# A limit in kilobytes for the loads in flight, shorter channel loads and earlier branch hints in a fused RWKV-5 and SwiGLU kernel

## The chip, the cores and the metric

The kernel runs on one core of one Trainium2 chip. The metric is the time of one execution on the device in microseconds (us); the table below gives the median of three runs.

## The reference, cut to what matters

The first half is a linear attention with a decaying state, for 4 batches, 8 heads, 768 tokens and 48 channels per head. The second half normalises each token's 384 features and puts them through a SwiGLU layer of width 1536. All is float32.

```python
for t in range(S):
    kt, vt, rt = (k[:, :, t], v[:, :, t], r[:, :, t])
    cur = np.einsum('bhd,bhe->bhde', u[None] * kt, vt)
    y[:, :, t] = np.einsum('bhd,bhde->bhe', rt, state + cur)
    state = w[None, :, :, None] * state + np.einsum('bhd,bhe->bhde', kt, vt)
...
rms = np.sqrt(np.mean(x * x, axis=-1, keepdims=True) + 1e-06)
xn = x / rms * rms_g
g = xn @ w_gate
silu = g * (1.0 / (1.0 + np.exp(-g)))
return (silu * (xn @ w_val) @ w_out).astype(np.float32)
```

## The kernel before, in words

The 768 tokens are cut into 12 chunks of 64 (`NS`, index s). For each chunk the kernel loads three arrays: `CH` holds r and k with channels on the partitions ("chan", loaded by `load_chan`), `TOK` holds r and k with tokens on the partitions (`load_tok`), and `V` holds v (`load_v`). Each has one buffer only, so that a load has to wait until the chunk before has been read. A chunk of attention (`mixing(s)` and `state(s)`) goes as follows. DVE decays r into `RR` and k in place (rows named R and K). TensorE forms the scores A from them (`products`), and in the first two chunks also E, from u times k, which ScalarE makes as `ku`. DVE writes the diagonal and the masked scores into `MT` (d and m). TensorE forms the outputs Y from `V`, `MT` and, from the second chunk on, the state `ST` and the decayed r. ScalarE keeps the outputs as `yT` and their squares as `sq`. The mean of the squares (r, `ms`), its root (POOL `pow`, DVE `inv`, `diag` and TensorE `spread` in the first two chunks) and the scaling (x) follow. U is the chunk's update of the state; it needs `KH`, which DVE makes from `TOK` and the table `wk`; ScalarE (first chunk) or DVE then brings it into `ST`.

Weights come as 64-bit words and are rounded to float32: a load on SP into one of six `raw` buffers, an `ulp` on ScalarE, two operations `bits` on DVE, and a sum on POOL (`piece`). Gate and value products then go through the three PSUM banks a, b and c. The first two chunks are multiplied plainly (`gate_val`, `project`); from the third on, two chunks together go through a seven-product scheme (`group`, `second_layer`). In this later part, 36 loads called "look" (`check`) read the weights once more into `rows_out` to test their low bits; ScalarE works on them.

Nothing here is left to a scheduler. `Plan` holds all 1536 operations, each with an engine, a cost and its dependencies; `ORDER` is one list written out by hand that says in which order they are issued, and so the order on every engine. The costs serve one thing only: `times` works out from them when TensorE would idle, and `warm` fills such gaps, in the first PE operations, with matmuls of `ones` into an unused bank, so that TensorE is not idle. Their number is a function of the planned gap. The first gap has a formula of its own:

```python
for _ in range(4 * int((until + 0.4 - 3.75) / 0.86)):
    pe.matmul(bank[:, 0, 0:P], ones, ones, start=True, stop=True)
...
for _ in range(int((until - since - 0.25) / 0.23)):
```

All loads stand in one queue, SP's, and are issued in order. `InOrder.at_most` (line 165) keeps four counted loads in flight: the fifth gets a wait on the landing of the oldest. The loads of `CH`, `TOK`, `V` and the raw weights are counted, the look loads and the stores are not.

At the end, a value computed on the chip (`bad`) is loaded into a register on each engine, and a branch (`tc.If` in `program`, line 1773) goes past the general version of the kernel, which is not needed for these inputs. `hint` marks the branch as likely taken, on each engine. It is called by `Plan.give` (line 231) ahead of the third-last TensorE operation, and each engine's hint stands after the last instruction that the engine has been given by then.

Of the kernel before, what the change touches and what calls it, by code (L numbers as in the profile page):

```python
# [49 lines left out]
P = 128  # L50
# [10 lines left out]
B, H, S, D = 4, 8, 768, 48  # L61
# [11 lines left out]
def feature_order():  # L73
# [10 lines left out]
    0, 6, 8, 42, 44, 5, 4, 7, 21, 11, 10, 41, 43, 16, 1, 2, 3, 45, 46, 47, 76, 12, 51, 48, 49, 52, 53, 55, 31, 36, 26,  # L84
    13, 14, 58, 50, 59, 15, 54, 17, 22, 60, 62, 65, 66, 100, 18, 19, 23, 24, 113, 9, 108, 103, 20, 67, 68, 83, 56, 27,
    61, 84, 63, 64, 57, 25, 69, 70, 38, 33, 39, 28, 71, 72, 124, 77, 86, 78, 126, 90, 29, 34, 118, 193, 85, 79, 87,
    30, 123, 80, 133, 32, 127, 125, 102, 81, 195, 82, 105, 106, 104, 37, 200, 128, 134, 35, 40, 107, 91, 131, 129,
    109, 114, 95, 130, 132, 92, 135, 119, 73, 110, 136, 96, 137, 155, 115, 111, 120, 116, 205, 210, 121, 139, 140, 97,
    138, 101, 93, 75, 74, 279, 112, 117, 141, 142, 143, 156, 150, 151, 157, 122, 98, 196, 163, 159, 160, 144, 197,
    198, 149, 145, 161, 206, 201, 164, 146, 199, 191, 274, 192, 284, 88, 152, 158, 162, 147, 148, 167, 218, 207, 202,  # L90
    165, 168, 169, 166, 203, 212, 213, 171, 172, 215, 170, 216, 208, 175, 176, 204, 209, 179, 180, 211, 177, 173, 217,
    174, 178, 183, 187, 89, 181, 182, 276, 219, 277, 153, 227, 275, 184, 188, 281, 194, 289, 280, 222, 282, 321, 311,
    306, 185, 225, 189, 247, 248, 249, 186, 214, 154, 190, 99, 278, 283, 251, 252, 255, 285, 250, 253, 254, 220, 256,
    257, 94, 238, 259, 263, 260, 264, 291, 286, 287, 288, 258, 267, 313, 308, 292, 314, 307, 224, 290, 228, 221, 271,
    316, 293, 261, 312, 268, 317, 265, 269, 223, 226, 309, 229, 331, 326, 336, 272, 266, 270, 262, 310, 315, 298, 302,
    294, 295, 242, 230, 322, 233, 234, 328, 355, 352, 318, 323, 299, 303, 296, 231, 300, 304, 297, 232, 353, 356, 235,
    236, 243, 327, 346, 319, 324, 305, 301, 329, 237, 244, 341, 273, 386, 390, 391, 387, 246, 354, 358, 245, 357, 320,
    325, 330, 332, 359, 362, 388, 392, 342, 333, 338, 334, 343, 344, 335, 339, 347, 337, 340, 345, 361, 364, 365, 348,
    360, 389, 375, 407, 349, 380, 363, 383, 381, 239, 393, 384, 500, 350, 366, 406, 394, 395, 351, 368, 369, 416, 437,
    367, 396, 241, 370, 501, 371, 382, 405, 404, 502, 398, 372, 399, 400, 373, 504, 503, 397, 438, 507, 509, 240, 374,  # L100
    376, 408, 378, 512, 377, 401, 402, 445, 409, 410, 385, 403, 413, 439, 446, 456, 457, 417, 441, 440, 447, 411, 442,
    462, 443, 444, 448, 451, 449, 463, 450, 464, 452, 453, 455, 454, 506, 458, 460, 465, 505, 459, 470, 467, 471, 466,
    468, 472, 508, 469, 473, 414, 415, 418, 590, 461, 422, 481, 474, 412, 476, 482, 510, 477, 478, 475, 483, 518, 591,
    513, 480, 484, 489, 485, 511, 479, 486, 490, 491, 487, 514, 488, 628, 492, 627, 519, 515, 520, 525, 493, 495, 624,
    526, 527, 496, 625, 497, 494, 521, 499, 528, 533, 523, 522, 530, 534, 419, 420, 423, 421, 424, 428, 524, 516, 517,
    425, 636, 529, 535, 498, 531, 544, 532, 626, 536, 634, 539, 598, 537, 545, 629, 540, 647, 541, 633, 538, 546, 543,
    547, 552, 635, 549, 548, 542, 550, 551, 630, 553, 631, 555, 554, 558, 632, 556, 563, 559, 560, 562, 565, 564, 557,
    567, 637, 426, 427, 429, 430, 566, 651, 568, 561, 571, 569, 570, 574, 582, 584, 575, 572, 573, 599, 577, 576, 578,
    638, 579, 434, 431, 583, 600, 595, 596, 601, 639, 581, 580, 592, 606, 585, 589, 593, 611, 432, 433, 588, 435, 586,
    602, 603, 587, 597, 436, 607, 642, 612, 643, 700, 640, 594, 747, 644, 701, 608, 615, 645, 756, 641, 652, 609, 610,  # L110
    646, 748, 614, 648, 649, 749, 616, 613, 617, 619, 618, 681, 744, 745, 650, 605, 653, 654, 621, 604, 682, 620, 657,
    746, 622, 683, 623, 660, 826, 689, 656, 684, 655, 685, 754, 690, 757, 753, 751, 691, 686, 706, 687, 688, 692, 695,
    693, 707, 708, 696, 697, 699, 709, 694, 702, 658, 703, 704, 714, 711, 698, 712, 715, 659, 661, 750, 662, 710, 663,
    705, 716, 717, 713, 725, 718, 755, 762, 719, 666, 720, 726, 827, 752, 727, 721, 723, 758, 722, 724, 728, 863, 733,
    860, 730, 664, 665, 763, 734, 729, 731, 732, 667, 669, 735, 736, 759, 760, 739, 864, 737, 769, 740, 771, 861, 741,
    770, 764, 765, 865, 743, 862, 772, 777, 866, 738, 766, 767, 670, 778, 668, 671, 774, 742, 773, 775, 780, 675, 779,
    776, 783, 834, 781, 867, 873, 782, 788, 784, 785, 790, 789, 835, 787, 791, 796, 793, 792, 786, 869, 797, 798, 794,
    795, 799, 802, 883, 800, 870, 676, 807, 803, 804, 806, 809, 808, 810, 801, 815, 812, 672, 673, 674, 677, 816, 768,
    761, 811, 805, 678, 888, 813, 818, 814, 821, 819, 817, 836, 831, 832, 871, 822, 823, 820, 872, 868, 825, 824, 828,
    829, 833, 874, 837, 843, 838, 679, 680, 844, 875, 839, 830, 878, 879, 847, 876, 841, 980, 981, 846, 877, 887, 880,  # L120
    842, 881, 845, 848, 851, 882, 884, 889, 886, 885, 984, 850, 891, 852, 890, 853, 919, 855, 849, 917, 918, 983, 920,
    982, 854, 856, 857, 990, 840, 858, 922, 921, 923, 924, 893, 859, 925, 892, 896, 931, 936, 926, 937, 927, 932, 933,
    928, 942, 929, 935, 944, 943, 945, 986, 938, 985, 939, 894, 930, 940, 934, 993, 895, 947, 950, 998, 987, 951, 946,
    948, 899, 1063, 941, 953, 952, 949, 954, 956, 961, 957, 1096, 958, 963, 962, 960, 964, 988, 992, 955, 965, 966,
    989, 969, 959, 967, 968, 972, 1097, 900, 897, 970, 898, 991, 975, 973, 976, 994, 901, 971, 1098, 905, 1001, 977,
    974, 979, 978, 999, 1005, 1000, 1007, 1006, 1003, 1013, 1008, 1002, 1010, 1009, 1011, 1012, 995, 1102, 1014, 1015,
    1070, 1016, 1019, 1017, 1105, 902, 903, 904, 908, 1062, 1024, 1020, 1021, 1119, 1023, 1026, 1025, 1027, 1018,
    1106, 1028, 1029, 1032, 1022, 1030, 1031, 1035, 1033, 1100, 1034, 1038, 1036, 1043, 1039, 906, 1103, 1040, 1045,
    1044, 1124, 1004, 1037, 909, 907, 911, 996, 1047, 1042, 1046, 1099, 1048, 1041, 1049, 1051, 1071, 1050, 1101,
    1109, 910, 1123, 1054, 1052, 1108, 1104, 1107, 997, 914, 1057, 1055, 1216, 1056, 1110, 1060, 1053, 1058, 1059,  # L130
    1061, 1064, 1072, 1111, 912, 1065, 1114, 1115, 1067, 1068, 1073, 1078, 1074, 1075, 1083, 1172, 1173, 913, 1069,
    1112, 1217, 1066, 1219, 915, 916, 1113, 1116, 1084, 1079, 1117, 1080, 1118, 1120, 1218, 1121, 1122, 1082, 1125,
    1126, 1087, 1229, 1076, 1088, 1086, 1089, 1091, 1085, 1155, 1127, 1153, 1154, 1077, 1128, 1156, 1093, 1094, 1158,
    1157, 1159, 1160, 1220, 1092, 1090, 1081, 1095, 1161, 1167, 1228, 1223, 1162, 1225, 1163, 1164, 1168, 1129, 1169,
    1226, 1165, 1171, 1174, 1221, 1234, 1177, 1299, 1178, 1132, 1180, 1298, 1166, 1222, 1179, 1175, 1176, 1186, 1170,
    1181, 1224, 1227, 1182, 1332, 1183, 1187, 1184, 1185, 1230, 1232, 1130, 1131, 1333, 1188, 1189, 1192, 1190, 1197,
    1193, 1135, 1335, 1194, 1199, 1198, 1235, 1191, 1196, 1200, 1205, 1195, 1202, 1203, 1133, 1134, 1206, 1201, 1138,
    1207, 1208, 1204, 1334, 1211, 1209, 1241, 1212, 1336, 1344, 1231, 1236, 1136, 1213, 1243, 1242, 1210, 1345, 1337,
    1237, 1215, 1244, 1214, 1249, 1238, 1239, 1246, 1245, 1250, 1251, 1247, 1248, 1137, 1139, 1140, 1144, 1252, 1255,
    1253, 1338, 1341, 1254, 1260, 1256, 1257, 1306, 1259, 1262, 1261, 1307, 1263, 1268, 1265, 1258, 1266, 1269, 1264,  # L140
# [18 lines left out]
class InOrder:  # L159


    def __init__(self, tc, engine):
        self.tc, self.engine, self.flying = tc, engine, []

    def at_most(self, n, give):


        made = give()
# [13 lines left out]
class Plan:  # L182
# [48 lines left out]
    def give(self, order, free, idle, hint, final):  # L231
# [4 lines left out]
        for i in order:  # L236
            if i == last[0]:
                hint()
# [9 lines left out]
def fast(ctx, tc, chan, tok, vpad, wka, wkb, wot, cols, u_row, out, bad):  # L248
# [12 lines left out]
    FIRST, IN_FLIGHT = 2, 4  # L261
# [1590 lines left out]
```

## Time and profile before

| What | Value |
|---|---|
| Time, median of 3 runs | 594.98 us (593.34 to 597.05) |
| Time of the profiled execution | 594.46 us |
| Its span, first to last instruction | 592.7 us |
| TensorE (PE) busy | 582.0 us, 98% |
| VectorE (DVE), ScalarE (ACT), GpSimd (POOL) busy | 415.3, 293.8, 41.9 us |
| Granted TensorE clock, mean | 0.998 |
| DMA, whole span | 62.99 MB, mean 106 GB/s |
| DMA, first 50 us | 14.99 MB, mean 300 GB/s |

The profile comes from one execution. "Busy" is the time in which an engine had at least one instruction running, so the filler matmuls count as busy too. In the profile every program matmul of float32 has two records, and two weight loads. A releaser, "<-", is what ended the idle time ahead of a row. Nearly all operations carry line 179, which is the wrapper that issues them, so the rows are told apart by the names of the tiles.

### The profile page before, as it was taken

What the parts mean: (1) busy time and instruction counts of PE and PEld (TensorE: products, weight loads), DVE (VectorE), ACT (ScalarE), POOL (GpSimd) and SP (SyncE); (2) the same over time, 40 slices, a digit from 0 to 9 for tenths busy, and PEclk for the clock granted to TensorE, in tenths of its full rate; (3) what the DMA queues carried; (4) which work ended last, traced back from release to release, by engine and by line L of the source; (5) the groups of instructions that cost most, each with busy time, mean ns of one, the idle gap of its engine ahead of it and who ended that gap; (6) DMA issues with size and microseconds to landing.
All of it is one profiled execution on the core that took longest, in us unless ns stands there. A gap on an engine that the chain in (4) does not pass through costs nothing.

```text
span 592.7 us, 16598 instructions
## 1 busy us (share of the span) xinstructions
PE 582.0 (98%) x7280; PEld 520.5 (88%) x7280; DVE 415.3 (70%) x622; ACT 293.8 (50%) x713; POOL 41.9 (7%) x40
## 2 busy tenths in 40 slices
PE   8999999999999999999999999999999999999996
PEld 7888887668888998888999889999889999988995
DVE  7888769595786977776795667795777585455641
ACT  5864458364366654564462474584365473124100
POOL 2443234100000000000000000000000000000000
PEclk9999999999999999999999999999999999999999
DMA  7975463412613123512222415301531200301002
GB/s 268 337 254 232 167 239 90 146 34 55 213 55 116 55 75 103 198 36 97 82 92 67 143 58 187 133 8 40 165 119 62 69 29 17 92 2 54 2 4 55
DMA packets 22768, 62.99 MB, mean 106 GB/s; under 512 B 2944, under 2 KB 9760, under 8 KB 21280
## 3 DMA queue, kind: packets, MB, share of 16 engines
q1 hardware_dynamic: 21920, 61.36, 30.8%
q8 instruction: 58, 0.95, 0.7%
q10 hardware_dynamic: 768, 0.49, 0.3%
q14 instruction: 22, 0.18, 0.1%
HBM read 56.04 MB, written 4.72 MB: 103 GB/s over the span
## 4 chain that ended last, share of the span: by engine, by line
PE 95%; DMA 2%; DVE 1%; issue 1%; ACT 0%; SPq 0%; POOL 0%; DVEq 0%
PE bank_b L179 33%; PE bank_c L179 27%; PE bank_a L179 27%; PE at L179 8%; DMA V<-in_vpad_dram 1%; DMA chan<-in_chan_dram 1%; DVE ms L179 0%; DVE KH L179 0%; ACT ku L179 0%; SPq L179 0%; ACT wk L179 0%; POOL ms L179 0%; ACT diag L179 0%; DVE rows_out L179 0%; DVE diag L179 0%
## 5 line engine op out<-in xcount | busy, mean ns | idle before, releaser
L179 DVE TENSOR_TENSOR gv<-bank_b,m 128x512 f32<-128x512 f32 x90 | 62.1, 690 | 63.5 <-PE bank_b L179 59.2
L179 ACT ACTIVATE gv<-gv 128x512 f32<-128x512 f32 (+1 forms) x60 | 30.8, 522 | 74.9 <-DVE gv L179 74.7
L179 DVE TENSOR_TENSOR gv<-bank_c,gv 128x512 f32<-128x512 f32 x60 | 41.4, 690 | 21.7 <-PE bank_c L179 21.2
L179 PE MATMUL bank_b<-xa,wa 64*128 64x256 f32 x444 | 55.3, 379 | 0.0
L179 PEld LDWEIGHTS bank_b<-xa,wa 64*128 64x128 f32 x444 | 43.2, 187 | 5.0 <-issue 0.7
L179 PE MATMUL bank_a<-xb,wb 64*128 64x256 f32 x372 | 46.5, 379 | 0.0
L179 PE MATMUL bank_a<-xa,wa 64*128 64x256 f32 x372 | 46.0, 378 | 0.0
L179 PE MATMUL bank_b<-t,s 64*128 64x256 f32 x360 | 45.2, 379 | 0.6 <-issue 0.6
L179 PE MATMUL bank_a<-wo,h 128*128 128x192 f32 x264 | 45.2, 327 | 0.0
L179 ACT ACTIVATE MT<-dmask,du 128x64 f32<-128x64 f32 x160 | 41.8, 336 | 6.1 <-DVE du L179 6.0
L179 PE MATMUL bank_b<-t,wb 64*128 64x256 f32 x360 | 44.6, 378 | 0.0
L179 PE MATMUL bank_c<-t,s 64*128 64x256 f32 x360 | 44.4, 376 | 0.0
L179 PE MATMUL bank_c<-xb,s 64*128 64x256 f32 x360 | 44.2, 376 | 0.0
L179 PEld LDWEIGHTS bank_a<-wo,h 128*128 128x128 f32 x264 | 43.2, 190 | 0.5
L179 ACT COPY m<-bank_a 128x512 f32<-128x512 f32 (+1 forms) x35 | 19.9, 568 | 47.7 <-PE bank_a L179 39.3
L179 ACT ACTIVATE gv<-bank_a 128x256 f32<-128x256 f32 x30 | 11.5, 382 | 58.6 <-PE bank_a L179 58.6
L179 PEld LDWEIGHTS bank_a<-xb,wb 64*128 64x128 f32 x372 | 36.3, 187 | 4.2 <-issue 0.3
L179 PEld LDWEIGHTS bank_b<-t,s 64*128 64x128 f32 x360 | 35.2, 187 | 5.4 <-issue 1.7
L179 PEld LDWEIGHTS bank_a<-xa,wa 64*128 64x128 f32 x372 | 36.4, 187 | 3.8
L179 ACT ACTIVATE rows_out<-rows_out 128x384 f32<-128x384 f32 x72 | 39.1, 554 | 0.5
L179 PEld LDWEIGHTS bank_c<-t,s 64*128 64x128 f32 x360 | 35.8, 187 | 3.5
L179 PEld LDWEIGHTS bank_c<-xb,s 64*128 64x128 f32 x360 | 35.5, 187 | 3.6
(189 smaller groups left out, 1099.3 us busy)
## 6 DMA issues: line engine op xcount, KB each, us to landing
chan<-in_chan_dram SPq DMA_DIRECT2D x11, 1024.0 KB, 5.4
TOK<-in_tok_dram SPq DMA_DIRECT2D x10, 768.0 KB, 4.7
V<-in_vpad_dram SPq DMA_DIRECT2D x12, 512.0 KB, 5.3
raw<-in_wot_dram SPq DMA_DIRECT2D x8, 576.0 KB, 5.0
rows_out<-in_wka_dram SPq DMA_DIRECT2D x12, 384.0 KB, 3.2
rows_out<-in_wkb_dram SPq DMA_DIRECT2D x12, 384.0 KB, 3.9
rows_out<-in_wot_dram SPq DMA_DIRECT2D x12, 384.0 KB, 3.4
raw<-in_wka_dram SPq DMA_DIRECT2D x6, 576.0 KB, 5.8
```

Of the source, the lines that this page charges most:

```text
L179: return lambda *args, **kwargs: self.tc.keep_in_program_order(give(*args, **kwargs))
```

## The change

1. **Limit in flight.** `at_most(4, ...)` becomes `within(1800, size, ...)`: each counted load carries its size in thousands of bytes, and a new load waits for the oldest ones until the sum, itself included, is at most 1800. Sizes: a chan piece of the first chunk 262, `TOK` 786 (or 393), `V` 524, a raw piece 393 or 590. The look loads are now counted too, each as 901.
2. **Channel rows.** From the second chunk on, chan is loaded as two transfers of 48 partitions (393 each) in place of one of 128 partitions; rows 48 to 63 of each half, which are padding, are left out. The planned cost of this load falls from 3.3 to 2.6.
3. **Branch hints.** TensorE's hint goes ahead of the 14th-last TensorE operation instead of the third-last; the hints of the other engines go to the middle of `ORDER`.
4. **Order.** `ORDER` is another permutation of the same operations, and the list of unused banks for the fillers is changed with it.

```diff
-    def at_most(self, n, give):
+    def within(self, limit, size, give):
         made = give()
-        self.flying.append(made.ins)
-        if len(self.flying) > n:
+        self.flying.append((made.ins, size))
+        while len(self.flying) > 1 and sum(x for _, x in self.flying) > limit:
             self.tc.add_manual_dep(
-                made.ins, self.flying.pop(0).name,
+                made.ins, self.flying.pop(0)[0].name,
...
-        last = [i for i in order if self.ops[i][0] == "PE"][-3:]
+        last = [i for i in order if self.ops[i][0] == "PE"][-14:]
+        middle = order[len(order) // 2]
         for i in order:
             if i == last[0]:
-                hint()
+                hint(mybir.EngineType.PE)
+            if i == middle:
+                hint(*(engine for engine in mybir.ALL_ENGINES if engine != mybir.EngineType.PE))
...
-    FIRST, IN_FLIGHT = 2, 4
+    FIRST, IN_FLIGHT = 2, 1800
...
     def load_chan(s):
-        sp.at_most(IN_FLIGHT, lambda: sp.dma_start(out=CH, in_=chan[s]))
+        for z in range(2):
+            rows = slice(64 * z, 64 * z + D)
+            sp.within(IN_FLIGHT, 393, lambda: sp.dma_start(out=CH[rows], in_=chan[s, rows]))
...
-            "SP", 0.95, [], keys, lambda: sp.dma_start(out=raw, in_=src[:, k * CHECK : (k + 1) * CHECK]), land=3*LAND,
+            "SP", 0.95, [], keys, lambda: sp.within(IN_FLIGHT, IN_FLIGHT // 2 + 1, lambda: sp.dma_start(out=raw, in_=src[:, k * CHECK : (k + 1) * CHECK])), land=3*LAND,
...
-    unused = list("baaaacbbbbbb")
+    unused = list("bbaaccbbbbbbbb")
...
-    def hint():
+    def hint(*engines):
         traced = nc.cur_bb.bb.instructions
-        for engine in mybir.ALL_ENGINES:
+        for engine in engines:
```

The built programs differ as follows. The matmuls of the computation are the same; the fillers fall from 31 program matmuls to 22 (12 in the first gap in both, 19 and 10 after it). The first loads on SP go from k1, r1, k0, r0, raw, raw, V to k0, r1, k1, r0, raw, V, raw, where r and k are the pieces of chan and the digit is the pair of batches q. On DVE the first R (of q1) goes ahead of the table `down`. On TensorE the second scores A of the first chunk go ahead of the first Y, and the second half of the product into bank b goes from after the second chunk's A to ahead of the first U. Program instructions from hint to branch: DVE 6 and 308, ACT 4 and 332, SP 5 and 85, POOL 2 and 2, PE 20 and 87 (before and after; a PE matmul makes four records).

## The prediction

> **What bounds the kernel now.** I read the page first. TensorE is busy for 98% of the span at full clock, and stays at 9 tenths or more in all but the first and the last slice.
>
> ```profile
> span 592.7 us, 16598 instructions
> PE 582.0 (98%) x7280; PEld 520.5 (88%) x7280; DVE 415.3 (70%) x622; ACT 293.8 (50%) x713; POOL 41.9 (7%) x40
> ...
> PE   8999999999999999999999999999999999999996
> ```
>
> So a change that leaves the matmuls alone can win only fillers, gaps at the start, and what follows the last matmul. The table by stretches says that PE is busy 8.72, 8.86, 8.96 and 9.26 of each 10 us up to 40, and then all of it but for 0.61 us near 354. The list of PE's waits is short; "issue" is a wait that the profile cannot explain.
>
> ```profile
> PE bank_b L179 <- DVE h L179: 1.1, 1, 1.1
> PE at L179 <- DMA V<-in_vpad_dram: 0.8, 1, 0.8
> PE at L179 <- issue: 0.7, 1, 0.7
> PE bank_a L179 <- issue: 0.7, 1, 0.7
> ```
>
> The timeline of PE shows where the start is lost (start, length, tiles, records):
>
> ```profile
> 7.04 0.71 PE L179 MATMUL bank_a<-ones 128*128 128x128 f32 x4
> 9.13 1.60 PE L179 MATMUL bank_a<-ones 128*128 128x128 f32 x12
> 11.54 0.91 PE L179 MATMUL at<-MT,V 64*64 64x64 f32 x48 [0.80 <-DMA V<-in_vpad_dram]
> 14.00 0.91 PE L179 MATMUL bank_c<-MT,V 64*64 64x64 f32 x48
> 24.57 1.15 PE L179 MATMUL at<-V,KH 64*64 64x48 f32 x64 [0.37 <-DVE KH L179]
> 31.20 0.57 PE L179 MATMUL at<-MT,V 64*64 64x64 f32 x23
> 32.52 0.81 PE L179 MATMUL at<-MT,V 64*64 64x64 f32 x41 [0.74 <-issue]
> ```
>
> The reader should see that PE is filled up, not needed, until about 25: Y of the first chunk waits for V, U for KH, and after Y of the second chunk (31.20) PE only runs its list. The time won at 31.20 is the time won at the end, if nothing stalls later.
>
> The chain of waits ends with PE until 586.83 and one DVE add until 587.22; the span ends 5.5 us later. The rows of the branch line show what lies there:
>
> ```profile
> L1773 SPq EVENT_SEMAPHORE  x8: 17/17/17, 590.8 to 591.4; - x8
> L1773 POOLq COMPARE_BRANCH  x1: 65/65/65, 561.6 to 561.6; - x1
> L1773 POOLq EVENT_SEMAPHORE  x1: 17/17/17, 563.9 to 563.9; - x1
> ...
> L1773 DVEq COMPARE_BRANCH  x1: 84/84/84, 586.9 to 586.9; - x1
> L1773 ACTq COMPARE_BRANCH  x1: 73/73/73, 587.8 to 587.8; - x1
> L1773 SPq COMPARE_BRANCH  x1: 70/70/70, 587.8 to 587.8; - x1
> L1773 ACTq EVENT_SEMAPHORE  x1: 17/17/17, 588.3 to 588.3; - x1
> L1773 DVEq EVENT_SEMAPHORE  x1: 21/21/21, 590.3 to 590.3; - x1
> ```
>
> From branch to next event ACT takes 0.5 us, POOL 2.3, SP 3.0 and DVE 3.4. SP is last, and the closing barrier takes 1.3 us more (591.4 to 592.7).
>
> [...] 58 instruction packets of 0.95 MB on one queue are 16.4 KB each, and three branches cost 2.3 to 3.4 us against 0.5. [...]
>
> **The change, part by part.** Times are of the profiled execution.
>
> *First loads.* Before, V was the seventh load and was issued at 6.30, held by the limit of four; it landed by 11.40. Now the four chan pieces and a raw piece make 4 x 262 + 393 = 1441, V would make 1965, so V waits only for the first piece (4.08, when the first ku started). The last chan piece was used at 7.03. From there to 11.40, two raw pieces and V landed: 1310 KB in 4.37 us, 300 KB/us. Now 917 KB are left: V lands at 7.03 + 3.06 = 10.1, 1.3 earlier.
>
> *First Y.* DVE ends `up` at 5.28; then R q1 0.82, `down` 0.68, K q0 0.68, R q0 0.75 end at 8.2. PE: E q0 from 7.05 (r0), E q1 from 7.7 (ku q1, 6.30 + 1.28), A q0 from 8.4 to 9.1. m q0 takes 0.76: 9.9. So the first Y starts at 10.1, held by V, for 11.54. DVE then has bits (0.34 + 0.56), d (0.75), m (0.78): the second Y starts at 12.2 instead of 14.00.
>
> *From ms to U.* Ahead of ms DVE has three more raw pieces, 3 x (0.35 + 0.56) = 2.7, and the third lands at 10.1 + 3 x 393/300 = 14.0; so ms is at 15.0, for 16.46. The win is not kept: ACT now has the ulp of the fifth raw piece ahead of the copy of rms, and that lands after two chan halves and one raw piece, at 14.0 + (786 + 786)/300 = 19.2. Then ulp 0.57, rms 0.37, ku 1.28, wk 1.07: KH starts at 22.5 for 23.08, and U at 24.0 for 24.57.
>
> *From U to Y of the second chunk.* U, then the copies into ST on ACT: from U to A took 2.76 before, so A is at 26.8 and ends at 27.9. Before, two products of 1.5 and 1.29 stood between A and Y; now one does: PE is at Y at 29.4. DVE: KH 1.44, bits 1.5, K 1.21, d 1.28, and m 1.36 end at 29.4. V of this chunk may start only after U (25.2 at the latest, with 2 x 590 KB ahead of it): 1704 KB at 300 to 350 KB/us, from 24.6, is 29.5 to 30.3. I take 29.8, for 31.20: 1.4 us won. The bound is 0.5 (V at 30.7) to 2.7 (V early and A not held).
>
> *Holes.* The 0.74 in the middle of that Y has no releaser; the DMA share is 0.95 to 1.04 there (27 to 33 us). If fewer bytes queue, it may go: 0 to 0.7, I take 0.4. A check: fillers after the first gap fall by 9 program matmuls, 18 records; the 38 such records took 5.52 us, so 18 are 2.6 us of gaps no longer planned. My 1.8 lies below, since raw pieces and V hold it.
>
> *Body.* Chan moves 262 KB less per load, 11 times, but DMA has 70% free there; 11 more issues are about 0.35 us each on SP, which waits 193.7 us for ACT's looks alone. Both are hidden. The look's new wait (a look lands 3.2 to 3.9 us after its issue) holds SP and what stands behind it, V above all. In the new order the shortest cover is V of the tenth chunk: about 9 us of PE work from its release to its use, for 18 before, and TOK ahead of it. 0.8 to issue, 2 to start, 1310/300 = 4.4: 7.2. It fits; if not, 1 to 2 us. The other moves exchange neighbours; PE's changes between 64-row, packed and full matmuls (0.2 each, 1.50 for 1.29) go from 84 to 83. Body: 0, bounds -0.6 (the hole at 354) and +4.
>
> *End.* [...] Now DVE has 308; SP has 85 and its waits, [...]. Then SP is ready at 588.3 and waits for the last stores, issued at 587.2: landing 1.9/2.3/3.9 us (shortest, median, longest) is 589.1 to 591.1, so 589.5, plus 0.1 for the last event, plus 1.3: 590.9 to 591.1 for 592.7. I take 1.3 won, bounds 0 and 1.8. POOL's gap stays, covered by 27 us of other work.
>
> **Sum.** 1.4 + 0.4 + 0 + 1.3 = 3.1 us: 594.46 becomes 591.4. The median lies 0.5 above that execution, so I predict 591.9.
>
> **Rivals.**
> 1. *The hints don't act* [...]: only the start is won, 1.8, so 593.2. For: POOL's hint came 458 us ahead and its gap was still 2.3. [...]
> 2. *Slower: [...].* [...] Price: [...] 3.4 (DVE) and 3.0 (as SP). DVE waits for PE 59.2/90 = 0.66 us per sum and ACT 34.2/30 = 1.1 per copy; the rest, 2.7 and 1.9, reaches PE: 4.6. With the start won and the end not, 594.98 - 1.8 + 4.6 = 597.8. It decides from 1.8 us of stall on. [...] Against: the hints of before cost no visible stall, [...].
> 3. *The start is DMA-bound more loosely*: V and raw pieces land as early as the planned gaps say, 2.7, with both holes gone (1.3) and 1.8 at the end: 5.8, so 589.2. For: fillers. Against: 300 KB/us is what the first 50 us held.
>
> **How the numbers follow.** My forecast 0.50, its own range 590.4 to 593.4; rival 1 0.22; rival 2, with stalls of the new order, 0.18; rival 3 0.10. From 589.3 to 597.6 leaves out half of rival 3 and rather over half of rival 2's upper part: under 2 in 10. One per cent, 5.9 us, is about what this measurement can tell from no change (its three runs span 3.7). Faster takes the tail of rival 3: 0.05. Slower takes repeated stalls of rival 2: 0.07. Same: 0.88.
>
> **What would show it.** Right: V's wait gone or at about 10.1; second-chunk Y at 29 to 30.5; PE ending near 585; SP's events after the branch beginning about 589 with DVE's gap at 0.5. Wrong: PE waits for DVE or ACT of over 1 us after 40, above all just after the middle; V waits near chunk 10; SP still 3 us behind its branch.

## The result, and the profile after

The changed kernel is slower, not faster. Over nine runs of each the median is 599.34 us (596.54 to 601.90) for 595.48 before; the ratio is 1.0075, with a 95% interval of 1.0049 to 1.0100. The prediction was 591.9 with a range up to 597.6, and called 1.3 us at the end and 1.8 at the start won. The profiled execution took 599.34 us, so it stands at the median. The page:

```profile
span 597.6 us, 16572 instructions
PE 583.8 (98%) x7262; PEld 518.5 (87%) x7262; DVE 416.3 (70%) x622; ACT 294.6 (49%) x713; POOL 42.2 (7%) x40
...
PE   8989999999999999999999999999999999999996
...
PEclk8999999999999999999999999999999999999999
```

The clock row of the kernel before was

```profile
PEclk9999999999999999999999999999999999999999
```

PE has 18 filler records fewer and is nevertheless busy 1.8 us longer; in the first slice its clock is granted in part only (0.81; the last row of the page), and 6.8 us at half clock are an estimated 3.4 us of lost work. The last matmul ends at 592.7, for 586.8 before: 5.9 us later. The list of PE's waits shows several that the kernel before did not have, three of them over 1 us, and the V wait nearly gone:

```profile
PE bank_b L179 <- DVE gv L179: 1.8, 2, 1.2
PE bank_c L179 <- ACT ku L179: 1.5, 1, 1.5
...
PE at L179 <- DVE chan L179: 1.1, 1, 1.1
...
PE at L179 <- DMA V<-in_vpad_dram: 0.2, 1, 0.2
```

The start, from PE's timeline (start, length, tiles, records):

```profile
1.15 5.15 PE L179 MATMUL bank_b<-ones 128*128 128x128 f32 x24 [1.15 <-DVE h L179]
7.79 0.69 PE L179 MATMUL bank_c<-chan,ku 48*64 48x64 f32 x32 [1.49 <-ACT ku L179]
...
12.70 1.50 PE L179 MATMUL at<-MT,V 64*64 64x64 f32 x48
14.13 2.27 PE L179 MATMUL bank_c<-ones 128*128 128x128 f32 x10
16.34 0.91 PE L179 MATMUL bank_c<-MT,V 64*64 64x64 f32 x48
...
27.92 1.15 PE L179 MATMUL at<-V,KH 64*64 64x48 f32 x64 [0.50 <-DVE KH L179]
28.89 1.13 PE L179 MATMUL bank_a<-chan,ku 48*64 48x64 f32 x64
31.12 1.16 PE L179 MATMUL at<-RR,chan 48*64 48x64 f32 x64 [1.10 <-DVE chan L179]
```

Two things are to be seen. Ten filler records take 2.27 us, where twelve took 1.60 before: PE's granted clock is 0.50 there, from about 9.2 to 16.0, after the idle 1.49 us ahead of the first scores E. And every step of the chain is late: the first Y at 12.70 (11.54 before, 10.1 predicted), the second at 16.34 (14.00; 12.2), U at 27.92 (24.57; 24.0), and Y of the second chunk at 33.99 (31.20; 29.8).

The end, from the rows of the branch line (first and last start in us):

```profile
L1778 SPq EVENT_SEMAPHORE  x8: 17/17/17, 594.2 to 596.2; - x8
...
L1778 DVEq COMPARE_BRANCH  x1: 84/84/84, 592.7 to 592.7; - x1
L1778 DVEq EVENT_SEMAPHORE  x1: 21/21/21, 593.3 to 593.3; - x1
L1778 SPq COMPARE_BRANCH  x1: 70/70/70, 593.6 to 593.6; - x1
```

DVE now takes 0.6 us from branch to event (3.4 before) and SP 0.6 (3.0). From the last matmul to the end of the span it is 4.9 us, for 5.9 before. So the hints won about 1.0, and PE's list lost 5.9.

### The profile page after: what moved, and what is told of

Read it like the earlier page. It is cut to its first block, busy times and chain, and to the rows that moved or that the text cites. A ratio compares the mean times of both kernels' runs of the same rounds, so it can differ in the third digit from the quotient of the medians.

```text
span 597.6 us, 16572 instructions
## 1 busy us (share of the span) xinstructions
PE 583.8 (98%) x7262; PEld 518.5 (87%) x7262; DVE 416.3 (70%) x622; ACT 294.6 (49%) x713; POOL 42.2 (7%) x40
## 4 chain that ended last, share of the span: by engine, by line
PE 86%; DMA 8%; DVE 3%; issue 1%; SPq 1%; ACT 1%; POOL 0%; DVEq 0%; ACTq 0%
PE bank_b L179 31%; PE bank_a L179 25%; PE bank_c L179 24%; PE at L179 6%; DMA raw<-in_wka_dram 3%; DMA TOK<-in_tok_dram 2%; DMA chan<-in_chan_dram 1%; DVE bits L179 1%; DMA raw<-in_wkb_dram 1%; SPq L179 1%; DVE TOK L179 0%; DVE h L179 0%; DVE gv L179 0%; POOL wa L179 0%; DVE ms L179 0%
## 5 line engine op out<-in xcount | busy, mean ns | idle before, releaser
L179 ACT ACTIVATE gv<-gv 128x256 f32<-128x256 f32 (+1 forms) x60 | 31.1, 521 | 74.5 <-DVE gv L179 74.2
L179 PEld LDWEIGHTS bank_b<-t,wb 64*128 64x128 f32 x360 | 34.7, 187 | 4.1
```

What stands on the lines that cost most here:

```text
L179: return lambda *args, **kwargs: self.tc.keep_in_program_order(give(*args, **kwargs))
```

## Where the new waits come from: the chan load

The table of DMA issues gives KB per transfer and the median us from issue to landing. Before, with chan as one load, and after, in halves:

```profile
chan<-in_chan_dram SPq DMA_DIRECT2D x11, 1024.0 KB, 5.4
```

```profile
chan<-in_chan_dram SPq DMA_DIRECT2D x22, 384.0 KB, 6.5
```

A half with fewer bytes takes longer than the whole, 6.5 us for 5.4. The table by stretches shows the rate around the last chan load of the changed kernel, behind which only a look load stands in the queue (the last two columns are the DMA engines' busy share and the GB/s moved):

```profile
435.00:436.00 1.00, 0.91 (x67) 0.76 (x56) 0.96 (x3) 0.00 (x0) 0.00 (x0) 1.00 1.02 205
436.00:437.00 1.00, 0.96 (x8) 0.88 (x10) 1.00 (x2) 0.00 (x0) 0.00 (x0) 1.00 1.09 180
437.00:438.00 1.00, 1.00 (x12) 0.91 (x10) 0.53 (x2) 0.00 (x0) 0.00 (x0) 1.00 0.88 164
438.00:439.00 1.00, 1.00 (x14) 0.89 (x12) 0.40 (x2) 0.62 (x3) 0.00 (x0) 1.00 0.95 146
```

The DMA engines' busy share is 0.88 to 1.09, and they move 146 to 205 GB/s. With chan as one load (first run below) the same place reads:

```profile
432.00:433.00 1.00, 1.00 (x16) 0.88 (x10) 1.00 (x2) 0.00 (x0) 0.00 (x0) 1.00 0.98 401
433.00:434.00 1.00, 1.00 (x12) 0.91 (x10) 0.37 (x2) 0.00 (x0) 0.00 (x0) 1.00 1.01 397
```

What it costs can be followed to PE. The first line is from the chain of waits of the changed kernel, the second from DVE's timeline, the third from PE's: chan lands 7.7 us after its issue, DVE stands 2.27 us for it, and the sums queued behind it on DVE make PE wait 1.18 us.

```profile
434.12 7.69 DMA chan<-in_chan_dram
```

```profile
441.91 1.22 DVE L179 TENSOR_TENSOR RR<-chan,up 128x1024 f32<-128x1024 f32 x1 [2.27 <-DMA chan<-in_chan_dram]
```

```profile
444.34 1.57 PE L179 MATMUL bank_b<-xa,wa 64*128 64x256 f32 x12 [1.18 <-DVE gv L179]
```

At about the same busy share (0.98 and 1.01 with one load) the rate was 0.36 to 0.52 of that of the whole load. No run here tells whether it goes by which partitions a load covers or by their mere number (48 for 128). The prediction had counted the halves as fewer bytes at an unchanged rate, an estimate of its author's; measured, they were a loss.

## The experiments

None of these kernels leaves out or changes a part of the computation. Over the runs the granted clock of PE varies between 0.989 and 1.000, and the time with it: over 67 runs of the kernel before the slope is 0.47 us for 0.001. So beside each ratio stands the mean clock over the kernel's runs, and the mean time brought to full clock, time − 590 us × (1 − clock). This last column is an estimate: 590 us is about PE's busy time, and the measured slope is smaller. By it the kernel before has clock 0.9965 and 593.9 us, and the changed one 0.9932 and 595.5. The kernel before was measured anew beside each group of runs (medians 595.15, 595.79, 595.34 and 595.36, mean clocks 0.9963, 0.9965, 0.9972 and 0.9973). So kernels of different groups are compared by their ratios; a difference of 0.001 in mean clock can come from the group.

| Kernel | Median, us | Ratio to before, 95% | Mean clock | At full clock, us |
|---|---|---|---|---|
| changed | 599.34 | 1.0075 [1.0049, 1.0100] | 0.9932 | 595.5 |
| changed, chan whole | 594.86 | 0.9991 [0.9973, 1.0009] | 0.9956 | 592.3 |
| before, chan in half rows | 599.18 | 1.0072 [1.0046, 1.0098] | 0.9961 | 596.7 |
| before, hints moved | 594.21 | 0.9976 [0.9956, 0.9997] | 0.9977 | 592.9 |
| changed, 16 fillers first | 599.39 | 1.0081 [1.0059, 1.0104] | 0.9943 | 596.4 |
| changed, chan cut between r and k | 594.51 | 0.9982 [0.9967, 0.9998] | 0.9952 | 592.1 |
| changed, second chunk's chan whole | 598.37 | 1.0044 [1.0024, 1.0064] | 0.9940 | 594.9 |
| chan whole, limit 2700 | 594.39 | 0.9976 [0.9960, 0.9992] | 0.9949 | 591.6 |
| chan whole, order of before | 595.62 | 1.0000 [0.9981, 1.0019] | 0.9961 | 593.4 |
| chan whole, 2700, gaps filled | 599.01 | 1.0057 [1.0035, 1.0079] | 0.9947 | 595.7 |
| changed, gaps filled | 603.16 | 1.0128 [1.0107, 1.0150] | 0.9938 | 599.5 |
| chan whole, 2700, order of before | 592.98 | 0.9954 [0.9937, 0.9970] | 0.9988 | 592.4 |
| changed, longer fillers | 597.76 | 1.0051 [1.0033, 1.0068] | 0.9963 | 596.1 |
| chan whole, 2700, longer fillers | 593.22 | 0.9980 [0.9961, 1.0000] | 0.9976 | 592.5 |

### Is it the chan rows?

**One part undone: chan whole.**

```diff
-        for z in range(2):
-            rows = slice(64 * z, 64 * z + D)
-            sp.within(IN_FLIGHT, 393, lambda: sp.dma_start(out=CH[rows], in_=chan[s, rows]))
+        sp.within(IN_FLIGHT, 786, lambda: sp.dma_start(out=CH, in_=chan[s]))
```

> The changed kernel with chan loaded in one transfer of 128 partitions from the second chunk on (counted as 786, so that the limit acts as in the changed kernel). Rows theory (a transfer to 48 partitions runs slowly, so that the two halves land later than the whole did, and hold raw, TOK and V behind them): the landing of chan falls from 6.5 us to about 5.5 in the median, the stretch of 13 to 18 us is back from 49-246 to about 300 GB/s, the 1.2 us wait of PE behind chan near 443 is gone, and the time falls by 1.5 to 3 us, to 596.5-598. Clock theory (the start is lost to a half-speed TensorE clock after PE's 1.5 us gap at 6.3): the clock still falls to 0.5 from about 9.6 us, and the time stays within 1 us of 599.3. Limit theory (bytes in flight hold TOK and V): same as the clock theory.

**One part alone: the half rows in the kernel before.**

```diff
-        sp.at_most(IN_FLIGHT, lambda: sp.dma_start(out=CH, in_=chan[s]))
+        sp.dma_start(out=CH[0:D], in_=chan[s, 0:D])
+        sp.at_most(IN_FLIGHT, lambda: sp.dma_start(out=CH[64 : 64 + D], in_=chan[s, 64 : 64 + D]))
```

> The kernel before, with the chan load of the second chunk on cut into two transfers of 48 partitions (only the second is counted among the four in flight). Rows theory: each half lands in 6 us or more, first-50-us traffic falls below 300 GB/s, PE waits appear before 60 us, and the time rises by 1 to 3 us over 595.5. Clock and limit theories: the time stays within 0.7 us of the kernel before.

Undoing the rows takes the ratio from 1.0075 to 0.9991 (599.34 to 594.86 us); the rows alone make the kernel before 4.0 us slower (595.15 to 599.18). Either way they account for the whole loss, and for more than was forecast (1.5 to 3 us and 1 to 3). As forecast, without the halves chan lands after 5.3 us in the median, and PE's wait of 1.18 us behind chan is gone.

**Partitions or number of transfers?** Two transfers again, cut between r and k, each over all partitions and with more bytes than a half.

```diff
-            rows = slice(64 * z, 64 * z + D)
-            sp.within(IN_FLIGHT, 393, lambda: sp.dma_start(out=CH[rows], in_=chan[s, rows]))
+            sp.within(IN_FLIGHT, 393, lambda: sp.dma_start(out=CH[:, z], in_=chan[s, :, z]))
```

> The changed kernel with the chan load still in two transfers, but cut between r and k, each over all 128 partitions (524 KB each, more bytes than the two of the change, which move 393 KB each). Theory that the 48 partitions of a half are what makes it slow: each transfer lands within 5.5 us, not 6.5, and the time is that of the whole load, 594.9 within 1. Rival, that two transfers in place of one are what costs (another issue, another entry in the limit): 599.3 within 1, with PE late at the first U (27.9) as in the changed kernel.

The median is 594.51, that of the whole load, and the table of issues reads:

```profile
chan<-in_chan_dram SPq DMA_DIRECT2D x22, 512.0 KB, 5.3
```

512 KB over 128 partitions land in 5.3 us, 384 KB over 48 in 6.5. The number of transfers costs nothing that can be seen (594.51 for 594.86 us with one); the partitions that each one covers do, by their place or their number.

**Start or later chunks?** Only the second chunk's chan is loaded whole.

```diff
+        if s == 1:
+            sp.within(IN_FLIGHT, 786, lambda: sp.dma_start(out=CH, in_=chan[s]))
+            return
         for z in range(2):
```

> The changed kernel with the chan load of the second chunk as one transfer of 128 partitions and the other ten in halves. Of the 4.5 us that the halves cost in all, the trace puts about 2 at the start (PE 1.8 to 2.4 us late by 41 us) and the rest in stalls later. Theory that both parts exist: 597.0 within 1. If nearly all of it came from the start (clock and all): 595.0. If from the later chunks: 599.

At 598.37 it lies between the forecasts for "both" and "later chunks". At full clock 594.9 stands against 595.5 and 592.3: by this estimate 2.6 of the 3.2 us belong to the ten later loads and 0.6 to the start. That the later loads cost is clear of the noise (1.0044 [1.0024, 1.0064] against 0.9991 [0.9973, 1.0009]); the share of the start is not (1.0075 [1.0049, 1.0100]).

### The hints

```diff
-        last = [i for i in order if self.ops[i][0] == "PE"][-3:]
+        last = [i for i in order if self.ops[i][0] == "PE"][-14:]
+        middle = order[len(order) // 2]
         for i in order:
             if i == last[0]:
-                hint()
+                hint(mybir.EngineType.PE)
+            if i == middle:
+                hint(*(engine for engine in mybir.ALL_ENGINES if engine != mybir.EngineType.PE))
```

> The kernel before with only the hints moved as in the change. Hint reading of the prediction [...]: DVE and SP leave the branch in about 0.5 us instead of 3.4 and 3.0, the span ends about 5 us after the last matmul instead of 5.9, and the time falls by about 0.9 us, to 594.6. Displacement rival [...]: PE waits for DVE or ACT of 2 to 3 us just after the hints, and the time rises by 2 to 5 us. If hints do nothing: 595.5 and gaps of about 3 us at the branch.

0.94 us faster than before (594.21 for 595.15), as forecast, and the interval leaves 1 out. DVE now takes 0.6 us from branch to event, as in the changed kernel, and SP 0.6 too (587.1 to 587.7):

```profile
L1776 DVEq COMPARE_BRANCH  x1: 84/84/84, 586.3 to 586.3; - x1
L1776 DVEq EVENT_SEMAPHORE  x1: 21/21/21, 586.9 to 586.9; - x1
```

### The limit and the order

**A wider limit** (`IN_FLIGHT = 2700`), chan whole.

> The changed kernel with chan as one load of 128 partitions, and the limit in flight at 2700 in place of 1800 (looks count half of it, so 1351). Theory that the limit costs nothing once chan is whole: 594.9 within 1. Rival, that the limit of 1800 holds up loads that PE then waits for (a TOK load stood behind a raw load until 49.3 in the changed kernel): 592 to 593.5. Rival on the other side, that a wider limit lets raw loads take the bandwidth from V and chan at the start: 596 or more.

**The order and filler banks of before**, chan whole, limit 1800, hints moved.

> The changed kernel with chan whole and with the order and filler banks of the kernel before: what differs from the kernel before is the limit in kilobytes and the hints alone. The hints are worth 0.9. Theory that limit and order are worth nothing each: 594.2. If the limit costs and the order hides it: 595.5 or more. If the new order is what loses and the limit wins: below 593.

**The same with the limit at 2700.**

> The order and filler banks of the kernel before, chan whole, hints moved, limit at 2700: beside the run with the limit at 1800 (595.6), which was not faster than before although the hints give 0.9 alone. Theory that the limit of 1800 holds loads up in that order: 594.3, the time with the hints alone. Rival, that the limit is worth nothing either way and 595.6 was scatter of the clock (0.9961): 594.2 to 595.6, with a time at full clock of 593.0 to 593.4 again.

In the new order 2700 against 1800 is not told apart (the intervals overlap). In the old order it is: 1.0000 [0.9981, 1.0019] against 0.9954 [0.9937, 0.9970], so with the limit of 1800 the kernel is about 2.7 us slower there, 1.0 of it at full clock. 595.62 is what was forecast if the limit costs; 592.98 lies below all forecasts for its run. Where the old order loses is not shown: in the profiled execution at 1800 (592.26 us) PE has no wait over 0.3 us after 33 us. The last kernel is the fastest of all, 592.98 us; it beats both the changed kernel and the one before. Whether it also beats the kernel before with nothing but the hints moved is not told apart. How a limit can cost is seen in SP's timeline of the changed kernel, where the TOK load stands until a raw load has landed, and PE later waits 0.6 us for what depends on it:

```profile
44.23 0.61 SPq L179 DMA_DIRECT2D raw<-in_wkb_dram  x1
49.30 0.33 SPq L179 DMA_DIRECT2D TOK<-in_tok_dram  x1
```

### The clock at the start

**More fillers in the first gap.**

```diff
-            for _ in range(4 * int((until + 0.4 - 3.75) / 0.86)):
+            for _ in range(4 + 4 * int((until + 0.4 - 3.75) / 0.86)):
```

> The changed kernel with four more filler matmuls in the first gap (16 instead of 12), so that PE is not idle from 6.3 to 7.8 us. Clock theory: the granted clock stays at 1.0 through 10 to 16 us (mean 0.998 instead of 0.993), the second Y of the first chunk starts 2 us earlier than 16.34, and the time falls by 1 to 2.5 us, to 597-598. Rows and limit theories: the start wins at PE but is handed back to the late raw, TOK and V loads, and the time stays within 0.7 us of 599.3.

No gain (599.39). The profiled execution fell to half clock all the same (mean 0.83 over 10 to 20 us), at 11.6 us, after PE had been idle for 1.33 us ahead of A. **Both gaps filled**: in addition six fillers ahead of the first scores A,

```diff
-            for _ in range(int((until - since - 0.25) / 0.23)):
+            for _ in range(6 if len(unused) == 11 else int((until - since - 0.25) / 0.23)):
```

first with chan whole and the limit at 2700:

> The changed kernel with chan as one load, the limit at 2700, and the two first gaps of PE filled: 16 filler matmuls instead of 12 in the first gap, 6 instead of none ahead of the first scores A. Over the runs so far the time follows the mean clock (about 0.5 us for each 0.001); brought to full clock by 590 us per unit, the whole-load kernel with the limit at 2700 stands at 591.6 and the kernel before at 593.9, but its mean clock over its runs is 0.9949, where the kernel before has 0.9965. Theory that the idle PE in the first 10 us (6.9 us busy, 8.7 before) makes the clock fall: with the gaps filled the mean clock is 0.9965 or more and the time 593.0 to 593.7, ratio about 0.996. Rival, that the clock falls for other reasons: clock 0.995, time 594.4.

and in the changed kernel itself:

> The changed kernel with nothing but the two first gaps of PE filled as in the run beside it (16 and 6 fillers). Its mean clock over nine runs is 0.9932, and brought to full clock its time is 595.5. Theory that its loss has two parts, PE's waits for data (1.6) and a clock that falls after PE was idle at the start (1.9): clock up to 0.9965, time 597.5. Rival, that the clock falls all the same, as it did with 16 fillers in the first gap alone (0.9943): 599.

Both forecasts failed by far: 599.01 and 603.16. The start is at full clock now (1.00 up to 40 us in both), but Y of the second chunk starts where it did without the added fillers (33.00 for 33.05, and 33.91 for 33.99), and PE stops later. PE's timeline of the first of the two (from 40.7 us on it is at half clock, in the mean 0.66 over 40 to 50 us; the 16 records of the third line took 1.95 us without the added fillers):

```profile
36.38 1.24 PE L179 MATMUL bank_b<-xa,wa 64*128 64x256 f32 x9
39.28 0.70 PE L179 MATMUL bank_b<-xa,wa 64*128 64x256 f32 x3 [1.66 <-issue]
39.91 2.88 PE L179 MATMUL at<-ones,sq 128*128 128x1 f32 x16
```

and of the second:

```profile
41.23 0.70 PE L179 MATMUL bank_b<-xa,wa 64*128 64x256 f32 x3 [2.70 <-issue]
```

The profile shows no releaser for such a stop, and it stands in the middle of a group of matmuls on the same tiles, so a wait for data is unlikely. Counting matmul records from the start, such stops stand after record 476, 603 and 4815 before the change, 730 after it (there between two groups), 731 with 16 fillers, and 221 and 731 in both kernels with the gaps filled. The steps between them are about multiples of 127.5 records (476 − 221 is 2 × 127.5, 4815 − 603 is 33 × 127.6). What stops PE there is not shown; the stops last 0.2 to 2.7 us. The places go by count, so more fillers bring such a place to another moment and another matmul. That this makes the stops longer is not shown: their length differs from one execution to the next. In the stretch of 34 to 38 us, ahead of the 1.66, the DMA engines' busy share is 1.00 to 1.04; whether that has to do with the stop is not shown either.

So the clock needed a test that keeps the count. **Longer fillers, none added**: 176 columns instead of 128 in the first gap, and the three fillers behind the first A put ahead of it.

```diff
-    ones = c_tile([P, P], "ones")
-    dve.memset(ones, 1.0)
+    wide_ones = c_tile([P, 176], "ones")
+    ones = wide_ones[:, 0:P]
+    dve.memset(wide_ones, 1.0)
...
-                pe.matmul(bank[:, 0, 0:P], ones, ones, start=True, stop=True)
+                pe.matmul(bank[:, 0, 0:n], ones, wide_ones[:, 0:n], start=True, stop=True)
...
-            for _ in range(int((until - since - 0.25) / 0.23)):
+            n = 176 if len(unused) == 11 else P
+            for _ in range({11: 3, 10: 0}.get(len(unused), int((until - since - 0.25) / 0.23))):
```

> The changed kernel with the same number of filler matmuls, 12 in the first gap at 176 columns instead of 128, and the three behind the first scores A put ahead of them, also at 176; nothing else differs, and all later PE instructions have the same place in the sequence. Theory that PE's idle time at the start lowers the clock: the first idle of 1.5 to 1.9 us and the one of 1.1 ahead of A go, the mean clock over the runs rises from 0.9932 to 0.9965 or more, the time falls from 599.3 to 597.5. Rival, that the clock falls later, behind holes in PE's sequence: clock 0.993 to 0.994, 599.

> The same fillers in the changed kernel with chan as one load and the limit at 2700, which ran at 594.4 with a mean clock of 0.9949 and stands at 591.6 when brought to full clock. Theory that the idle start lowers the clock: clock 0.9965 to 0.998, 592.8 to 593.7. Rival: 594.4 at 0.995. If the longer fillers delay the first scores by more than they save: 595 or more with the clock up.

597.76 with a mean clock of 0.9963, and 593.22 with 0.9976: clock and median came as the theory said, within 0.3 us and 0.0002. But the kernel before also had a higher clock in this group (0.9973), and beside it the gain in time is not told apart: the ratio goes from 1.0075 [1.0049, 1.0100] to 1.0051 [1.0033, 1.0068], and from 0.9976 [0.9960, 0.9992] to 0.9980 [0.9961, 1.0000]. In the changed kernel with longer fillers the idle time ahead of E is 0.17 us, and the second Y starts at 13.74 instead of 16.34:

```profile
1.20 6.13 PE L179 MATMUL bank_b<-ones 128*128 128x176 f32 x24 [1.20 <-DVE h L179]
7.50 0.69 PE L179 MATMUL bank_c<-chan,ku 48*64 48x64 f32 x32 [0.17 <-ACT ku L179]
...
13.74 1.23 PE L179 MATMUL bank_c<-MT,V 64*64 64x64 f32 x48
```

At full clock this kernel is no faster than the changed one (596.1 for 595.5), so what its median gains would be the clock.

The rival, that the clock falls behind stops in PE's sequence, is not excluded. In the profiled execution of the second kernel PE is not idle ahead of E, and yet it runs at half clock from about 16.6 to 20.0 (mean 0.83 over 10 to 20 us), after a wait of 0.49 us at 11.55 and a stop of 0.47 us behind record 221:

```profile
14.51 0.90 PE L179 MATMUL bank_c<-MT,V 64*64 64x64 f32 x43 [0.47 <-issue]
...
16.82 2.93 PE L179 MATMUL bank_a<-yT,wa 64*128 64x128 f32 x24
```

The fifteen profiled executions have nine such stretches ahead of the last matmul, each about 3.4 or 6.8 us long. Six began within 2.6 us after PE had been idle for 1.3 to 2.7 us, one with an idle time of 1.1 us, and two after stops of only 0.47 and 0.28 us. On the other hand 1.36 us ahead of A (chan cut between r and k) and 1.92 us between 150 and 200 (changed, gaps filled) brought none (1.00 in the mean). So by the mean clocks (0.9932 to 0.9963 and 0.9949 to 0.9976 with longer fillers) an idle start makes half clock likelier; no length of idle time decides it here.

## Why the prediction was wrong

**The failed step** is in "Body": "Chan moves 262 KB less per load", and then "Both are hidden". The 262 KB less per load were counted, but not the rate at which the rest moves. The prediction priced chan by bytes at 300 KB/us, so a half of 384 KB would have been 1.3 us of transfer; the engines moved 146 to 205 GB/s. "DMA has 70% free there" did not help either: the share is a mean over the span, and during a half it is 0.88 to 1.09. Alone the rows cost 4.0 us, the upper end of the step's own bounds (−0.6 to +4). That the bound held is luck: it was drawn from a late V, and no rival carried this cause. A second step failed besides: the 1.8 us at the start were not won by any kernel here (0.2 at best), as the next parts show.

**First loads, first Y.** V was to wait for the first piece of chan, at 4.08; it was issued at 5.68, since that piece landed later. It nevertheless landed at 10.14, the predicted 10.1, by two errors that cancel: the last piece of chan landed at 7.65, where 7.03 was assumed, and the 917 KB behind it then took 2.5 us instead of 3.06. Such sums count a load behind all those issued ahead of it; that this holds was not shown. ScalarE's timeline shows the first use of chan:

```profile
5.75 2.56 ACT L179 ACTIVATE ku<-chan,col 128x128 f32<-128x128 f32 x8 [3.46 <-DMA chan<-in_chan_dram]
```

Over all kernels here, ku starts at 3.97 to 4.13 in the five with the old order and at 4.65 to 5.75 in the ten with the new one, whatever the limit. So it goes with the order; why, with pieces of one size, stays open. The prediction let E start at 7.05, with the fillers ending at 6.3 unchecked. PE stood 1.49 us and went to half clock (0.50), and the first Y then waited not for V but for PE's own list. In the profiled executions here the clock fell after idle times of 1.3 to 2.7 us, and after less (0.28 to 1.1). By the mean clocks, 0.9932 for 0.9965, an estimate of the clock's part in the loss is 590 × 0.0033 = 1.9 us; the start alone shows less, since with longer fillers Y of the second chunk moves from 33.99 to 33.07. The gap ahead of E, which the plan did not show, was left without cover.

**From ms to Y of the second chunk.** Predicted 29.8, measured 33.99. The terms before it were late by nearly 4 us (ms 18.80 for 15.0, U 27.92 for 24.0), while the steps themselves were about right: 9.1 us for 9.0 from ms to U, 3.2 for 2.8 from U to A. But half rows and clock are not the whole reason. With chan whole, in an execution at full clock, ms is at 15.93, U at 25.29 and this Y at 31.24, against 31.20 before. There A of the first chunk starts at 9.36 instead of 8.4, held 1.10 us by DVE's R, and that delay goes through the chain. So the gain of 1.4 did not come even there; the best start of this Y in any kernel here was 30.97.

**Holes.** The stop of 0.74 in that Y is gone, as said, and one of 0.49 came at 41.2: such stops stand at fixed counts of matmul records (730 for this one), as shown above. The 0.4 us is not a property of the change.

**Limit.** "The look's new wait" was priced at 0, bounded by 1 to 2 us. In the old order the limit of 1800 cost about 2.7 us against 2700. The place named, V of the tenth chunk, does not appear in PE's list of waits. What the changed kernel shows is TOK behind a raw load at 43 to 49, worth 0.6 us; what costs in the old order stays open. The limit of 1800 alone, with everything else as before, was not tried.

**End.** Right in that the moved hints act, on SP as well (85 instructions). What makes a hint act is not shown; that SP's would do so was an estimate. The rows show only that 0.6 us go with 85 and 308 instructions between hint and branch, 3.0 to 3.4 with 5 and 6, and 2.3 to 2.6 with POOL's 2, while ACT takes 0.5 with 4 and 332. The size was 1.0 in the profiled execution and 0.9 in the medians instead of 1.3: SP's events wait for the stores from 594.2 to 596.2, which is 3.5 us behind the last matmul, where 2.8 were predicted. POOL's gap stayed (2.6), as said.

**Rivals.** Rival 1 (hints don't act) falls by DVE's and SP's 0.6 us. Rival 2 (stalls of DVE and ACT behind the hints, priced at the 3.4 and 3.0 us of the branch rows) came nearest in time (597.8), with the wrong cause; where and how often they would stall was an estimate. After the hints at 266.7 to 269.3 PE has no wait until 444, where it is the one behind chan, and the hints alone are faster. Rival 3 falls with the start.

In sum, medians: half rows +4.5 (of which 1.4 is clock), hints −0.9, and order with limit together +0.6 (594.86 against 594.21), which lies within the scatter; predicted for them was −1.8.

## What to carry to other kernels

Before a load is split or trimmed, look at which partitions each piece covers: a cut along the free dimension was free (5.3 us for each 512 KB over 128 partitions), a cut into partition halves made each piece slower than the whole (6.5 us for 384 KB over 48, 5.4 for 1024 KB over 128). Give a load's price as bytes over the rate of its own shape (here 146 to 205 GB/s for 397 to 401), and check the cover at the place with the least of it, not by a mean share. When fillers are to keep the clock up, try longer ones before more of them. Here ten more filler matmuls cost about 4 us, while longer ones left every later instruction at its place in the sequence and the mean clock rose (0.9932 to 0.9963); a gain in time beyond the noise was not shown.

## What the runs showed of the hardware that was not expected

- Loads of 48 partitions moved 146 to 205 GB/s at a mean busy share of the DMA engines of 0.88 to 1.09, and a load of 128 partitions 397 to 401 at 0.98 and 1.01.
- The clock fell to half for about 3.4 or 6.8 us in seven of fifteen profiled executions ahead of the last matmul, six of nine times after PE had been idle for 1.3 to 2.7 us, once after 1.1, twice after 0.28 and 0.47; with 1.92 us idle it stayed at 1.00. So the mean clock of a kernel tells more than one profile.
- PE's stops of 0.2 to 2.7 us without a releaser, where they were counted, stood multiples of about 127.5 matmul records apart, at the same counts in different kernels (221, 476, 603, 731; once 4815), most of them in the first 45 us, where the DMA engines' busy share was 0.71 to 0.95 in the kernels before and after (0.27 and 0.31 from 60 us on).
- A branch hint 308 (DVE) and 85 (SP) instructions ahead brought 3.4 and 3.0 us from branch to event down to 0.6; the one 2 instructions ahead, on POOL, left 2.3 to 2.6. ACT took 0.5 us with its hint 4 and 332 instructions ahead.
